# The last products of a two-branch FFT kernel, cut into eight tiles of the array (one core)

## The chip, the cores and the metric

The kernel runs on one core of a Trainium2 chip. The metric is the device time of one execution in microseconds (us), the median over runs. Everything is float32; inputs start in DRAM and the output ends there.

## The reference

`x` has 2048 time steps and 640 channels. Two branches are mixed by a gate with one value for each time step:

```python
def _A_ref(u, log_A_real, A_imag, C_real, C_imag, log_dt, D_skip):
    ...
    K = 2.0 * jnp.einsum("dn,dnl->dl", C, P).real
    L2 = 2 * L
    u_t = u.transpose(0, 2, 1)
    Kf = jnp.fft.rfft(K, L2)
    Uf = jnp.fft.rfft(u_t, L2)
    y = jnp.fft.irfft(Uf * Kf[None, :, :], L2)[:, :, :L]
    ...
    return y + u * D_skip[None, None, :]

def _B_ref(x, w_r, w_i):
    X = jnp.fft.rfft2(x, axes=(-2, -1)) * (w_r + 1j * w_i)
    return jnp.fft.irfft2(X, s=(S, D), axes=(-2, -1))

x = A_u
g = _sigmoid((x * gate_w).sum(-1, keepdims=True))
a = _A_ref(x, ...)
b = _B_ref(x, B_w_r, B_w_i)
return g * a + (1 - g) * b
```

Branch A is a causal convolution over time with a filter of 2048 taps for each channel (`P` holds exponentials of 128 modes), done by FFTs of length 4096. Branch B is a two-dimensional FFT filter over time and channels.

## The kernel before, in words

All FFTs are products with tables on TensorE, in two stages. The channels are taken in four quarters of 160, called `c`. Time is 32 blocks of 64 steps, so that an inverse transform ends with a small product: for each of the 64 steps of a block, the 32 blocks come from 64 rows (real and imaginary parts of the odd frequencies of a 64-point transform) or from 32 rows (the even ones).

**Ahead of the change** stand the phases up to about 440 us. `phase_a` transforms `x` over time and leaves its spectrum in DRAM (`u_d`), forms the gate (`T.gate`: partition, kind, 16 values), and filters branch B, which it leaves one product short in DRAM as `s3e_d[c]`, 32 rows of 64 steps by 160 channels. `phase_p` and `phase_b` compute the filter `K` beside it (products `p_k`, L690, whose tiles are 128 rows by 32 columns), and leave it in `k_d`.

**`phase_d`** is where the change lies. It loops over the quarters `c` = 0 to 3 and in each over five groups `g` of the 33 frequency pairs (four, four, four, four and one; in the last quarter the single one comes fourth). The program hands several streams of instructions to `merge`, which deals them out by their estimated costs, so that the order on each engine is fixed when the program is built. The streams of one step are:

- `mains` (4.8): load a group of the spectrum (`us`, on ScalarE's queue); `fronts`: stage 2 of the filter's transform (`p_s`, L345), then VectorE multiplies out of PSUM (`ma` L792, `mb` L793) and VectorE and GpSimd add the halves into `t2` (L797, L798); `backs`, two groups behind (one behind in the last five): the first inverse stage (`p_i`, L811), ScalarE's copy to `s3` (L813, L815), and the stores to DRAM `s3_d[c]` (L817 for the one row `s3_d[c, 33]`, L820 for the others, on ScalarE's queue).
- `some(fst, ...)` (2.1): stage 1 of the next quarter's filter (`p_s`, L332), copied by ScalarE (L333), with its loads (`load_k`).
- what stands beside (2.4 for each): `last_e(c, a)` and `last_c(c - 1, a)`, for `a` = 0 and 8, in the groups that the loop names. `last_e` finishes branch B for eight of the 16 steps that lie beside each other in a row: the product `p_e` of `t3e` with the table `T.e3e` (the helper `halved`, L157), then VectorE multiplies by 1 - g into `oe` (L872). `last_c` finishes branch A: the product `p_c` of `t3` with `T.e3` (L889), then VectorE multiplies by g into `ot` (L894) and GpSimd adds `oe` (L895). In the last quarter VectorE does both in one (L892).

The data of these products come back from DRAM. `load_e` (L851, SyncE's queue) brings `s3e_d[c]` as 128 rows: 32 rows times four groups `r` of 16 steps. `load_c` (L862, SyncE's queue but for one) brings rows `p` to `p + n` of `s3_d[c]` as 2n rows: each row times two halves `j` of 32 steps. In the first three quarters it is called with n = 32, in the last with n = 16, and the final one in two parts.

The tables `e3` (128 by 64) and `e3e` (128 by 128) are block diagonal: 128 rows meet 64 columns, and each column has values for 64 or 32 of the rows and zeros for the others. A step of eight is worked in pieces of three, three and two (480, 480 and 320 columns of data); a piece is two matmuls, one to each half of PSUM's partitions, into a slot of `pd` (two slots of one bank). `ps` (three slots of two banks) serves all the other products of `phase_d`.

`behind(T.mm)` places a product after the latest `p_i` matmul in the order. After the loop come the remaining `backs`, the last loads of `t3`, `last_c` of quarters 2 and 3, and the stores of the output (`out`, L897 on GpSimd's queue, L900 and L950 on SyncE's). On the host `_lay_back` brings the output into its order.

## Time and profile before

| what | value |
|---|---|
| time, three runs | 620.0, 618.89, 628.3 us; median 620.0 |
| the profiled execution's own time | 619.24 us |
| its span, first to last instruction | 617.4 us |
| mean granted TensorE clock | 0.955 |
| busy PE (matmul), PEld (weight load) | 537.5 us (87%), 407.1 us (66%) |
| busy DVE, ACT, POOL | 506.9 us (82%), 391.3 us (63%), 268.5 us (43%) |
| DMA | 101.98 MB in 47987 packets, mean 165 GB/s |

The shares are those of the whole span; `phase_d` fills its last 180 us or so. The page's slices and the rows of a stretch show the limits of that stage, which are others than those of the phases ahead. In the rows quoted below, PE is TensorE's matmul, PEld its weight load, DVE VectorE, ACT ScalarE, POOL GpSimd, SP SyncE; an ending q names an engine's queue. A float32 matmul leaves two records, one for each of its passes, so that a `x4` of PE in the chain or the timeline is two matmuls. "128*64" is the tile of the array that a matmul uses, rows by columns; "128x480" is data, partitions by elements. A group's line shows count, busy time and mean ns of one, then the idle time before its instructions and what ended it. Buffer numbers are left out of names there.

### The profile page before, as it was taken

What the parts mean: (1) busy time and instruction counts of PE and PEld (TensorE: products, weight loads), DVE (VectorE), ACT (ScalarE), POOL (GpSimd) and SP (SyncE); (2) the same over time, 40 slices, a digit from 0 to 9 for tenths busy, and PEclk for the clock granted to TensorE, in tenths of its full rate; (3) what the DMA queues carried; (4) which work ended last, traced back from release to release, by engine and by line L of the source; (5) the groups of instructions that cost most, each with busy time, mean ns of one, the idle gap of its engine ahead of it and who ended that gap; (6) DMA issues with size and microseconds to landing.
All of it is one profiled execution on the core that took longest, in us unless ns stands there. A gap on an engine that the chain in (4) does not pass through costs nothing. (4 is left out here: it accounts for less than half of the span.)

```text
span 617.4 us, 16697 instructions
## 1 busy us (share of the span) xinstructions
PE 537.5 (87%) x7084; PEld 407.1 (66%) x7084; DVE 506.9 (82%) x788; ACT 391.3 (63%) x659; POOL 268.5 (43%) x246
## 2 busy tenths in 40 slices
PE   8688979978978979989899989998789989998874
PEld 6577657756665757676667766666667768787641
DVE  5961798799799978998999998778297886986954
ACT  6667675566866777798699897799735324333110
POOL 4921262053346255365336335235253437456441
PEclk9889989979989998998999989899999999999978
DMA  8776203235612321333233032105966989899996
GB/s 339 301 289 230 88 7 137 76 109 200 242 56 66 96 85 25 94 120 124 76 108 95 2 125 79 48 26 158 333 242 225 302 218 370 243 282 289 251 240 212
DMA packets 47987, 101.98 MB, mean 165 GB/s; under 512 B 3220, under 2 KB 32680, under 8 KB 46152
## 3 DMA queue, kind: packets, MB, share of 16 engines
q1 hardware_dynamic: 24792, 67.74, 33.7%
q10 hardware_dynamic: 20080, 22.52, 11.7%
q0 software_dynamic: 3040, 10.65, 5.2%
q8 instruction: 56, 0.92, 0.6%
q14 instruction: 19, 0.16, 0.1%
HBM read 60.91 MB, written 39.98 MB: 163 GB/s over the span
## 5 line engine op out<-in xcount | busy, mean ns | idle before, releaser
L676 POOL TENSOR_TENSOR y<-e,sc 128x512 f32<-128x512 f32 x40 | 57.9, 1447 | 123.0 <-issue 61.7
L345 PE MATMUL p_s<-t,w 128*64 128x160 f32 x1056 | 88.5, 308 | 11.8 <-ACT t L333 4.2
L345 PEld LDWEIGHTS p_s<-t,w 128*64 128x64 f32 x1056 | 74.6, 140 | 21.1 <-ACT t L333 5.7
L637 ACT ACTIVATE e<-p_e 128x512 f32<-128x512 f32 x120 | 68.5, 601 | 24.1 <-PE p_e L635 21.8
L333 ACT COPY t<-p_s 128x512 f32<-128x512 f32 x40 | 44.7, 1141 | 61.5 <-PE p_s L332 43.3
L548 PE MATMUL p_eo<-td,pmt 107*128 107x321 f32 x204 | 68.9, 462 | 3.7 <-ACT pmt L502 3.7
L690 PE MATMUL p_k<-x,y 128*32 128x64 f32 x2560 | 61.9, 228 | 10.0 <-DVE x L675 5.4
L690 PEld LDWEIGHTS p_k<-x,y 128*32 128x32 f32 x2560 | 45.3, 113 | 37.5 <-issue 30.7
L649 DVE SCALAR_TENSOR_TENSOR q<-q,p_p 128x512 f32<-128x512 f32 x80 | 52.9, 680 | 12.4 <-ACT q L648 10.9
L635 PE MATMUL p_e<-rm,par 128*128 128x512 f32 x120 | 57.4, 510 | 4.1 <-ACT e L637 2.2
L677 POOL TENSOR_TENSOR y<-e,sc 128x512 f32<-128x512 f32 x40 | 55.2, 1380 | 4.4 <-ACT sc L663 4.4
L797 POOL TENSOR_TENSOR t<-ma 64x320 f32<-64x320 f32 x32 | 28.3, 883 | 64.0 <-DVE ma L792 52.7
L646 PE MATMUL p_p<-rp,par 128*128 128x512 f32 x80 | 44.5, 566 | 9.6 <-DVE q L649 9.4
L548 PEld LDWEIGHTS p_eo<-td,pmt 107*128 107x128 f32 x204 | 38.7, 199 | 19.8 <-ACT pmt L502 6.8
L811 PE MATMUL p_i<-t,w 128*64 128x160 f32 x528 | 45.0, 305 | 4.7 <-POOL t L798 3.2
L648 ACT ACTIVATE q<-p_p 128x512 f32<-128x512 f32 x80 | 46.4, 595 | 2.7 <-PE p_p L646 2.5
L332 PE MATMUL p_s<-c,u 128*64 128x128 f32 x640 | 44.2, 284 | 3.5 <-ACT ut L379 2.8
L332 PE MATMUL p_s<-c,kt 128*64 128x128 f32 x640 | 43.4, 275 | 3.9 <-DVE mb L793 1.6
L332 PEld LDWEIGHTS p_s<-c,kt 128*64 128x64 f32 x640 | 38.3, 137 | 13.0 <-issue 5.9
L792 DVE TENSOR_TENSOR ma<-p_s,us 128x640 f32<-128x640 f32 (+1 forms) x36 | 28.2, 783 | 21.9 <-PE p_s L345 14.1
L811 PEld LDWEIGHTS p_i<-t,w 128*64 128x64 f32 x528 | 38.2, 139 | 9.6 <-POOL t L798 4.1
L332 PEld LDWEIGHTS p_s<-c,u 128*64 128x64 f32 x640 | 36.8, 140 | 11.3 <-issue 5.1
(154 smaller groups left out, 1206.2 us busy)
## 6 DMA issues: line engine op xcount, KB each, us to landing
u_d<-ut SPq DMA_DIRECT2D x32, 320.0 KB, 2.7
us<-u_d ACTq DMA_DIRECT2D x16, 640.0 KB, 7.1
s_d<-s ACTq DMA_DIRECT2D x15, 640.0 KB, 8.6
t<-s_d SPq DMA_DIRECT2D x6, 1280.0 KB, 9.6
ww<-in_w_l SPq DMA_DIRECT2D x8, 642.0 KB, 3.9
ue<-u_d SPq DMA_DIRECT2D x8, 640.0 KB, 4.5
k_d<-kt SPq DMA_DIRECT2D x4, 1280.0 KB, 7.0
kt<-k_d SPq DMA_DIRECT2D x8, 640.0 KB, 6.4
```

Of the source, the lines that this page charges most:

```text
L332: nc.tensor.matmul(p[64 * ri:64 * ri + 64, j, :], src(i + j), e1[ri], start=True, stop=True)
L333: copy(dst[:, :, :, i:i + n], p[:, 0:n, :].rearrange("p q (j k) -> p j k q", j=4))
L345: ins = nc.tensor.matmul(p[64 * j:64 * j + 64, i, 160 * ri:160 * ri + 160], w2[:, x, 64 * ri:64 * ri + 64], t1[:, x if x < 32 else K0, :], ...
L548: P.matmul(p[:, :E], st.pmt[:DC, c, w, j, :], tv[:DC, w, c, :], start=c == 0, stop=c == 2)
L635: P.matmul(p[:, :], pars[t], rm[:, c:c + 512], start=True, stop=True)
L637: st.exp = S.activation(ef[:, c:c + 512], p[:, :], AF.Exp)
L648: S.activation(qf[:, c:c + 512], p[:, :], AF.Copy, bias=MAGIC)
L649: V.scalar_tensor_tensor(out=qf[:, c:c + 512], in0=qf[:, c:c + 512], scalar=MAGIC, in1=p[:, :], op0=ALU.subtract, op1=ALU.subtract)
L676: G.tensor_tensor(out=y[:, 1], in0=e[:, :, 64:96], in1=sc[:, 0], op=ALU.mult)
L677: G.tensor_tensor(out=y[:, 0], in0=e[:, :, 64:96], in1=sc[:, 1], op=ALU.mult)
L690: P.matmul(st.pb[32 * r:32 * r + 32, o, :], y[:, ri, 4 * qq + JR[r], :], x[:, ri, 4 * qq + JR[r], :], start=t % 2 + qq + 1 - ri == 0, stop ...
L811: T.mm = P.matmul(p[x:x + 64, i // 2, 160 * (i % 2):160 * (i % 2) + 160], T.w3[:, k0 + h + i, x:x + 64], t2[:, h + i, :], start=True, stop ...
```

## The change

The last two products use the array in eight tiles at once. A tile is 64 rows (branch A) or 32 rows (branch B) by 32 columns.

- The tables lose their zeros: `e3` and `e3e` are now 32 columns wide, and hold the same 64 rows twice and the same 32 rows four times.
- A new function `product` issues eight matmuls of 320 columns for a piece: for each of four column slots `s` (32 of PSUM's partitions) and two halves `j` (a bank each) the rows of half `j`, steps 4s + v and 4s + v + 1. A piece `v` = 0 or 2 gives 640 elements in each partition; a step of eight is two pieces, not three.
- `p_l`, the product's PSUM slot, comes from `ps`, which has four slots of two banks now. `pd` is gone.
- VectorE multiplies a whole piece (128 by 640) at once; in the last quarter it still works by 160.
- The halves `j` lie on partitions 0 to 63 and 64 to 127 of `t3` now (before: two neighbouring partitions for each row). So each load of `load_c` becomes two DMAs, one for each `j`, of n rows; `load_e` becomes four DMAs of 32 rows.
- The output's partitions are now (s, block) instead of (x, j, block), so `_lay_back`, the gate's copy and the views `four` and `gate` follow. The stores of the last quarter are one whole and two pieces of 320 KB, where they were one whole, one of six steps and one of two before.
- `yield 0.8` becomes `yield 1.2` in both streams, which shifts how `merge` deals them out.

```diff
-    e3 = np.zeros((64, 2, 2, 32))
-    for j in range(2):
-        e3[:, j, j, :] = kr
-    e3e = np.zeros((32, 4, 4, 32))
-    for r in range(4):
-        e3e[:, r, JR[r], :] = kr[32:64]
+    e3, e3e = np.tile(kr, (2, 1)), np.tile(kr[32:64], (4, 1))
...
-    y = y.reshape(4, 2, 2, 32, 16, 160)
-    return np.ascontiguousarray(y.transpose(3, 2, 1, 4, 0, 5).reshape(1, L, D))
+    y = y.reshape(4, 4, 32, 2, 2, 4, 160)
+    return np.ascontiguousarray(y.transpose(2, 4, 3, 1, 5, 0, 6).reshape(1, L, D))
...
-def halved(nc, out, w, x):
-    for i in (0, 64):
-        nc.tensor.matmul(out[i:i + 64], w[:, i:i + 64], x, start=True, stop=True)
...
-        T.e3, T.e3e, T.id, T.one = take(64), take(128), take(128), take(32)
+        T.e3, T.e3e, T.id, T.one = take(32), take(32), take(128), take(32)
...
-            V.tensor_copy(T.gate[32 * r:32 * r + 32, 0, :], p[32 * r:32 * r + 32, 16 * JR[r]:16 * JR[r] + 16])
+            o = slice(32 * r, 32 * r + 32)
+            V.tensor_copy(T.gate[o, 0, :].rearrange("p (x j v) -> p x j v", x=2, j=2), p[o].rearrange("p (j x s v) -> p x j s v", j=2, x=2, s=4)[:, :, :, r])
...
-    ps = ctx.enter_context(tc.tile_pool(name="c_ps", reuse_waits="tile", bufs=3, space=PSUM))
-    pd = ctx.enter_context(tc.tile_pool(name="d_ps", reuse_waits="tile", bufs=2, space=PSUM))
+    ps = ctx.enter_context(tc.tile_pool(name="c_ps", reuse_waits="tile", bufs=4, space=PSUM))
...
-        nc.sync.dma_start(t3es[c][:, :, :], T.s3e_d[c].rearrange("k (r a) d -> (k r) a d", r=4))
+        for r in range(4):
+            nc.sync.dma_start(t3es[c][32 * r:32 * r + 32], T.s3e_d[c, :, 16 * r:16 * r + 16])
...
-        src = T.s3_d[c, p:p + n].rearrange("k (j x a) d -> (k j) x a d", x=2, j=2)
-        w = 16 // parts
-        for a in range(0, 16, w):
-            T.ld = eng.dma_start(t3s[c][2 * p:2 * p + 2 * n, :, a:a + w], src[:, :, a:a + w])
+        src = T.s3_d[c, p:p + n].rearrange("k (j x a) d -> j k x a d", x=2, j=2)
+        for x in range(parts):
+            w = slice(x, x + 1) if parts > 1 else slice(0, 2)
+            for j in range(2):
+                T.ld = eng.dma_start(t3s[c][64 * j + p:64 * j + p + n, w], src[j, :, w])
+    def product(w, t, x, v, rows):
+        p = ps.tile([128, 2, 512], F32, tag="ps", name="p_l")
+        with behind(T.mm):
+            for s in range(4):
+                for j in range(2):
+                    r = slice(64 * j + rows[0], 64 * j + rows[1])
+                    P.matmul(p[32 * s:32 * s + 32, j, 0:320], w[r, :], t[r, 4 * s + v:4 * s + v + 2, :], start=True, stop=True)
+        return p[:, :, 0:320].rearrange("p j (v d) -> p j v d", v=2)
...
-        for i in range(0, AG, 3):
-            n = min(3, AG - i)
-            p = pd.tile([128, 3, 160], F32, tag="pd", name="p_e")
-            with behind(T.mm):
-                halved(nc, p[:, 0:n], T.e3e, t3es[c][:, a + i:a + i + n])
-            V.tensor_tensor(out=oe[:, i:i + n], in0=p[:, 0:n], in1=gate(1, a + i, n), op=ALU.mult)
-            yield 0.8
+        x = a // AG
+        for v in (0, 2):
+            p = product(T.e3e, t3es[c], x, v, (32 * x, 32 * x + 32))
+            V.tensor_tensor(out=four(oe, v), in0=p, in1=gate(1, a, v), op=ALU.mult)
+            yield 1.2
...
-        for i in range(0, AG, 3):
-            n = min(3, AG - i)
-            p = pd.tile([128, 3, 160], F32, tag="pd", name="p_c")
-            with behind(T.mm):
-                for x in range(2):
-                    P.matmul(p[64 * x:64 * x + 64, 0:n], T.e3, t3[:, x, a + i:a + i + n], start=True, stop=True)
+        x = a // AG
+        for v in (0, 2):
+            p = product(T.e3, t3[:, x], x, v, (0, 64))
...
-                V.tensor_tensor(out=ot[:, i:i + n], in0=p[:, 0:n], in1=gate(0, a + i, n), op=ALU.mult)
-                (V if c == 2 and a and n < 3 else G).tensor_tensor(out=ot[:, i:i + n], in0=ot[:, i:i + n], in1=oe[:, i:i + n], op=ALU.add)
-            if c < 2 and i + n == AG:
+                V.tensor_tensor(out=four(ot, v), in0=p, in1=gate(0, a, v), op=ALU.mult)
+                (V if c == 2 and a and v else G).tensor_tensor(out=four(ot, v), in0=four(ot, v), in1=four(oe, v), op=ALU.add)
+            if c < 2 and v:
                 G.dma_start(out[c, :, a:a + AG], ot[:, :, :])
-            elif c == 3 and i + n > (5 if a else 6):
-                x = i if a and i > 3 else 0
-                nc.sync.dma_start(out[c, :, a + x:a + i + n], ot[:, x:i + n])
-            yield 0.8
+            elif c == 3 and (v or a):
+                o = out[c, :, a:a + AG]
+                if a:
+                    nc.sync.dma_start(four(o, v), four(ot, v))
+                else:
+                    nc.sync.dma_start(o, ot[:, :, :])
+            yield 1.2
```

In the changed file `stage1` is L320, stage 2 L333, `p_i` L799, the products of `product` L866, `load_e` L845, `load_c` L857, the stores of `s3` L805 and L808, ScalarE's copies of it L801 and L803.

TensorE's order, a stretch in the middle of `phase_d` in which quarter 0's results are finished beside quarter 1's groups. The rows name the tiles `p_s` (both stages of the filter's transform), `p_i` (inverse stage) and `p_c` (branch A's product); a count is in matmuls here. Before:

```order
L345 MATMUL p_s_6280<-t_5652,w_68 64x160 x7
L889 MATMUL p_c<-t_6071,c_65 64x480 x2
L345 MATMUL p_s_6280<-t_5652,w_68 64x160
L889 MATMUL p_c<-t_6071,c_65 64x480 x2
L332 MATMUL p_s_6302<-c_65,kt 64x128 x8
L811 MATMUL p_i_6313<-t_6075,w_5306 64x160 x8
L889 MATMUL p_c<-t_6071,c_65 64x320 x2
L811 MATMUL p_i_6329<-t_6075,w_5306 64x160 x8
```

The three pieces of a step are single pairs of matmuls, each in one place. The same stretch now, with `p_l` for the product's tile:

```order
L333 MATMUL p_s_6284<-t_5652,w_68 64x160 x8
L866 MATMUL p_l<-t_6090,c_65 32x320
L320 MATMUL p_s_6313<-c_65,kt 64x128 x8
L333 MATMUL p_s_6323<-t_5652,w_68 64x160 x8
L320 MATMUL p_s_6340<-c_65,kt 64x128 x8
L799 MATMUL p_i_6351<-t_6095,w_5306 64x160 x8
L866 MATMUL p_l<-t_6090,c_65 32x320
L799 MATMUL p_i_6373<-t_6095,w_5306 64x160 x5
L866 MATMUL p_l<-t_6090,c_65 32x320 x14
L799 MATMUL p_i_6373<-t_6095,w_5306 64x160 x3
L333 MATMUL p_s_6392<-t_5652,w_68 64x160 x2
L866 MATMUL p_l<-t_6090,c_65 32x320 x8
```

The two products of a step have one matmul early and the other seven together, in the middle of another block of `p_i`. Counted over the loop, the rows of `p_l` form 28 groups. After the loop the remaining ones stand together.

SyncE's queue of DMAs from quarter 1's loads of `t3` to the end. Before:

```order
L862 DMA t_6495<-s_d 64x5120 x2
L851 DMA t3e<-s3e_d 128x2560
L862 DMA t_6894<-s_d 64x5120 x2
L862 DMA t_6975<-s_d 32x5120 x2
L862 DMA t_6975<-s_d 32x2x1280 x2
L950 DMA out<-ot 128x1280 x2
L900 DMA out<-ot 128x1280
L900 DMA out<-ot 128x960
L900 DMA out<-ot 128x320
```

The loads of `t3` go to 64 rows, those of the last quarter to 32, `t3e` to all 128. Now:

```order
L857 DMA t_6549<-s_d 32x5120 x4
L845 DMA t3e<-s3e_d 32x2560 x4
L857 DMA t_6983<-s_d 32x5120 x4
L857 DMA t_7074<-s_d 16x5120 x4
L857 DMA t_7074<-s_d 16x2560 x4
L955 DMA out<-ot 128x1280 x2
L905 DMA out<-ot 128x1280
L903 DMA out<-ot 128x2x320 x2
```

The order of the transfers stays; a load of 64 rows has become two of 32, one of 32 two of 16, one of 128 four of 32. On ScalarE's queue the rows stay as they were; its last DMA, 32 rows of `t3`, has become two of 16.

15 lines of the change are left out of this document (10 added, 5 removed).

## Prediction

> **What bounds** the kernel now. I read the stretches first: busy time of PE, DVE and the rest, TensorE clock, DMA share and GB/s.
>
> ```profile
> 480.00:500.00 20.00, 18.33 (x244) 14.98 (x242) 19.27 (x26) 7.11 (x8) 9.88 (x11) 1.00 0.87 247
> 520.00:540.00 20.00, 18.16 (x236) 14.82 (x238) 17.63 (x24) 7.28 (x9) 10.68 (x12) 1.00 0.91 286
> 560.00:580.00 20.00, 16.36 (x195) 12.98 (x196) 17.76 (x24) 4.00 (x6) 10.73 (x12) 1.00 1.00 295
> 580.00:600.00 20.00, 15.90 (x148) 10.86 (x146) 13.80 (x22) 4.35 (x7) 7.53 (x9) 0.83 0.95 235
> 600.00:617.40 17.40, 8.80 (x36) 2.52 (x32) 7.42 (x21) 0.00 (x0) 4.38 (x4) 0.86 0.67 208
> ```
>
> The columns after the length are PE, PEld, DVE, ACT and POOL. Until 580 us three resources are almost full together: PE has 16.4 to 18.3 of 20 us, DVE 17.6 to 19.3, the DMA engines 0.87 to 1.00. None can give back much alone. From 580 on PE and DVE thin out and the DMA engines stay at 0.95. The chain that ended last says who decides there:
>
> ```profile
> 575.53 10.79 DMA s_d<-s
> ...
> 587.72 6.40 DMA s_d<-s
> ...
> 597.11 2.77 DMA s_d<-s
> ...
> 599.94 5.88 DMA t<-s_d
> ...
> 605.95 3.96 PE p_c L889 x12
> ```
>
> From 575.5 to 605.8 the path is mostly transfers: stores of `s3` to DRAM (`s_d`), then the load of the last quarter of `t3`. A store takes 2.77 us for half a tile alone, but 10.79 and 6.40 us for whole ones while `t3` loads run. So two prices matter: the products on PE and DVE before 594 us, and the loads after 575 us.
>
> **The products on PE.** Today's costs, from the chain inside the loop and from the groups by line:
>
> ```profile
> 537.27 0.87 PE p_s L332 x16
> ...
> 539.23 0.81 PE p_e L157 x4
> ...
> 541.99 0.54 PE p_e L157 x4
> ```
>
> ```profile
> L889 PE MATMUL p_c<-t,c 128*64 128x480 f32 (+1 forms) x96 | 25.7, 602 | 8.5 <-DVE t L798 3.8 <-DMA t<-s_d 3.7 <-PE p_c L889 0.6
> L157 PE MATMUL p_e<-t3e,c 128*64 128x480 f32 (+1 forms) x96 | 21.9, 529 | 4.6 <-DVE oe L872 4.6
> L690 PE MATMUL p_k<-x,y 128*32 128x64 f32 x2560 | 61.9, 228 | 10.0 <-DVE x L675 5.4 <-issue 2.1 <-ACT kt L698 1.8
> ```
>
> Four records (two matmuls, two passes each) of 480 columns hold PE 0.81 us, of 320 columns 0.54 us. One step of eight channels costs 0.81 + 0.81 + 0.54 = 2.16 us. Each line has 96 records, so eight such steps. Twelve of the sixteen stand inside the loop: 25.9 us.
>
> After, a run of up to eight matmuls of 320 columns should cost 0.54 us if all eight overlap, 1.08 us for a step. But the order splits them. Counting the rows of `L866` inside the loop gives 31 runs (fourteen in a row count as two) in 28 groups with `128*64` matmuls around them. The runs cost 31 x 0.54 = 16.7 us. Each group changes the array's tiles twice. A change of that kind stands in the trace where `p_k` (32 columns wide) stands between `p_s` (64):
>
> ```profile
> 432.88 1.09 PE L332 MATMUL p_s<-c,kt 128*64 128x128 f32 x16 [0.34 <-ACT t L333]
> 433.90 1.10 PE L690 MATMUL p_k<-x,y 128*32 128x64 f32 x64
> 435.06 2.06 PE L332 MATMUL p_s<-c,kt 128*64 128x128 f32 x32
> ```
>
> Sixteen `p_s` records need 0.87 us from start to next start; here 433.90 - 432.88 = 1.02, so 0.15 us is lost on the way in. The `p_k` row is 1.10 us long with its last record's 0.22 (mean 228 ns), so `p_s` could follow after 0.88; it follows after 1.16: 0.28 us. I take 0.4 us of these 0.43 for a round trip, since the second may hold a short wait. 28 x 0.4 = 11.2 us. PE inside the loop: 16.7 + 11.2 - 25.9 = +2.0 us. If changing tiles were free it would be -9.2; if the row tiles did not overlap, 16.7 more than my value. No row shows row tiles overlapping; four column tiles do, since 64 `p_k` records go by in 0.88 us, 14 ns each. I take the overlap.
>
> **The products on DVE.**
>
> ```profile
> L792 DVE TENSOR_TENSOR ma<-p_s,us 128x640 f32<-128x640 f32 x32 | 26.3, 821 | 21.4 <-PE p_s L345 14.1 <-issue 5.7 <-POOL t L798 1.3
> L872 DVE TENSOR_TENSOR oe<-p_e,gate 128x480 f32<-128x480 f32 x16 | 10.5, 657 | 0.5
> L894 DVE TENSOR_TENSOR ot<-p_c,gate 128x480 f32<-128x480 f32 x12 | 7.9, 655 | 11.4 <-PE p_c L889 9.0 <-issue 2.1
> L892 DVE SCALAR_TENSOR_TENSOR ot<-p_c,gate,oe 128x160 f32<-128x160 f32 x16 | 5.0, 377 | 5.8 <-PE p_c L889 5.7
> L872 DVE TENSOR_TENSOR oe<-p_e,gate 128x320 f32<-128x320 f32 x8 | 3.8, 481 | 0.0
> L894 DVE TENSOR_TENSOR ot<-p_c,gate 128x320 f32<-128x320 f32 x6 | 2.9, 488 | 3.7 <-PE p_c L889 3.7
> ```
>
> The gate multiplications fall from 42 to 28, each of 640 elements. `ma`, also 640 out of PSUM, takes 0.821: 28 x 0.821 = 23.0 us for 10.5 + 7.9 + 3.8 + 2.9 = 25.1, so -2.1 us. With both engines full I let both count: +2.0 - 2.1 = 0 for the loop. POOL's additions become fewer and longer under 11 us of 20 busy: nothing; on a critical add it would be well under 1 us.
>
> **The PSUM ring.** Five slots (three of two banks, two of one) become four of two banks shared by all. PE's wait for `oe`, 4.6 us, may vanish. Against that, where the first matmul of two products is issued early (three places), they hold two of four slots for some five blocks of about 1 us, and PE may wait for one evacuation, about 1 us, once or twice: up to +4. I take 0.
>
> **The loads.** Bytes stay, the rows of each transfer change, and the rate depends on them (last column, GB/s):
>
> ```profile
> 452.00:454.00 2.00, 0.94 (x18) 0.97 (x20) 1.97 (x4) 0.00 (x0) 1.66 (x2) 1.00 1.01 425
> 541.50:544.50 3.00, 3.00 (x44) 2.63 (x42) 2.94 (x5) 2.26 (x3) 1.55 (x2) 1.00 1.08 218
> 602.50:603.50 1.00, 0.00 (x0) 0.00 (x0) 0.79 (x2) 0.00 (x0) 1.00 (x2) 1.00 0.98 195
> 606.50:608.50 2.00, 2.00 (x8) 0.54 (x4) 0.65 (x3) 0.00 (x0) 0.00 (x0) 0.50 1.00 417
> ```
>
> In 452:454 `t3e` and `us` load to 128 rows, in 606.5:608.5 128 rows are stored: 417 to 425. In 541.5:544.5 a `t3` load goes to 64 rows, in 602.5:603.5 the last ones to 32: 218 and 195, with the engines just as busy. So half the array's rows halve the rate, and a quarter costs no more.
>
> `t3e` now comes as four loads of 32 rows: 1280 KB need 6.2 us at 213 GB/s, not 3.1, four times.
>
> ```profile
> 519.64 19.25 SPq L862 DMA_DIRECT2D t<-s_d  x2
> ...
> 542.57 0.33 SPq L851 DMA_DIRECT2D t3e<-s3e_d  x1
> ```
>
> ```profile
> 566.53 0.97 PE L157 MATMUL p_e<-t3e,c 128*64 128x480 f32 x4
> ```
>
> ```profile
> ACT s L813 <- DMA s_d<-s: 8.2, 2, 5.2
> ```
>
> The load issued at 542.57 is first read at 566.53, 24 us later, which hides 3.1 us. What it could reach are the stores beside it, and ACT waited for stores only twice, both after 575 us: 0, at most +3 if that cover goes. The two halves of a 64-row `t3` load become a low and a high pair of 32 rows, one behind the other: same rate if the engines keep step, better if they drift; 0, at best -2.
>
> The last channel's `t3` loads fall from 32 rows to 16 + 16. No row shows 16. Between the rates of 32 rows (195 to 213, no loss) and half of them (107, if the next halving costs what the first did) a 640 KB load takes 3.1 to 6.2 us. By the nearest row alone it is 3.1; I take the middle, 4.7, because one of two known halvings did cost. Two of these loads run while the store of 587.72 waits, and that store lies on the path: ACT's next store writes a DRAM row of the same range, so ACT stands until it lands, and behind it queue the last three stores, two evacuations and a load. 2 x 1.6 = +3.1 us, between 0 and +9 (the second rival). The final loads, 5.88 us on the chain: +1, between 0 and +2.
>
> The Trainium skill, page SBUF — State Buffer, section Door 1: The DMA port swizzle, says that rows 0 to 31 and 0 to 63 both reach 8 of 16 ports, as the trace has it, and rows 0 to 15 only 4, with 104 GB/s measured; no run here shows 16 rows. By it alone the sum would be the second rival's.
>
> **The finish.** DVE sets it:
>
> ```profile
> 607.85 0.97 DVE L892 SCALAR_TENSOR_TENSOR ot<-p_c,gate,oe 128x160 f32<-128x160 f32 x3 [4.53 <-PE p_c L889]
> 609.40 1.55 DVE L892 SCALAR_TENSOR_TENSOR ot<-p_c,gate,oe 128x160 f32<-128x160 f32 x5 [0.57 <-PE p_c L889]
> 611.53 2.59 DVE L892 SCALAR_TENSOR_TENSOR ot<-p_c,gate,oe 128x160 f32<-128x160 f32 x8 [0.58 <-PE p_c L889]
> ```
>
> ```profile
> out<-ot SPq DMA_DIRECT2D x1, 480.0 KB, 2.6
> out<-ot SPq DMA_DIRECT2D x1, 160.0 KB, 2.3
> ```
>
> PE starts at 605.95 and DVE at 607.85. At the slow clock of that moment a product takes about 1.1 us, so DVE starts near 607.25, and then has 0.97 + 1.55 + 2.59 = 5.1 us without a gap: 612.4 instead of 614.1, -1.7. The last store grows from 160 to 320 KB: +0.3 at most.
>
> **Sum.** The profiled execution took 619.24 us (span 617.4). 0 (loop) + 3.1 + 1 (loads) - 1.7 + 0.3 = +2.7: 622 us. The execution lies 0.8 us under the runs' median of 620.0, so as a ratio this is 1.00. Two per cent, 12.4 us, is about what a measurement of this kernel tells from no change (its runs spread from 618.9 to 628.3).
>
> **Rivals.** First, gain: changing tiles costs far less than 0.4 us. PE gives back up to 9.2 us in the loop, DVE 2.1; DVE's 17.6 to 19.3 of 20 leave room for about half, 5 to 6, and with -1.4 at the end and no loss in the loads it is 612. For it: the chain holds `p_e` and `p_c` again and again. Against: the two rows above, and the split products.
>
> Second, the starved store, slower: 16-row loads at 107 GB/s take 6.2 us. The place is the store of 587.72. The first load runs from about 588, the second stands right behind it in the same queue before the store is through, and the store gets its turn only after both: 588 + 12.4 + 2 = 602.5 instead of 594.1, +8.4; final loads +2, finish -1.4: 628. It decides from the point where the second load is queued before the first ends. For it: 10.79 us for the first store, behind `t3`. The skill's page above, by its 104 GB/s, gives this rival.
>
> Third, row tiles do not overlap: +16.7 in the loop, 639. The Trainium skill, page TensorE: Matmul & The Clock Gate, Part 3, reports row and column tiles running at once; no run here shows it, and by it this rival falls.
>
> **Chances.** 622 (616 to 627) 0.52; starved store 0.27; gain 0.15; no overlap 0.06. Range 611 to 631: it cuts off half of the gain, the end of the starved store and the third rival. Slower by over 2% (above 631.6): 0.12; faster (below 606.8): 0.04; within: 0.84.
>
> **What would show it.** PE records of `p_l` a few ns apart in eights, about 0.54 us from group to group: overlap right. About 0.15 us lost before and 0.28 us after each group: switching right. GB/s near 210 while `t3e` loads, and 105 to 160 under the 16-row loads. The second-last whole store taking 9 to 10 us instead of 6.40. The last DVE instruction about 6.5 us after the first `p_l` of the last eight. I am wrong if the loop (first `p_e` to the end of the last `p_i`) shortens by over 5 us, or if the stores after 575 us are no slower than now.

## The result, and the profile after

The changed kernel takes 643.58 us (median of 6 runs, 636.12 to 651.88); the kernel before took 624.57 us in the runs beside it. The ratio is 1.030, with a 95% interval from 1.020 to 1.040. The forecast was 622 us, no change, with a range that ended at 631. The change makes the kernel slower by 3%.

The profiled execution takes 636.12 us with a span of 634.3 us. The phases ahead of the change took as long as before: the first `ma` starts at 445.3 us, before at 444.9. All of the difference, 189.0 - 172.5 = 16.5 us, lies in `phase_d`. First its stretches, as in the prediction (length, then PE, PEld, DVE, ACT, POOL, TensorE clock, DMA share, GB/s):

```profile
480.00:500.00 20.00, 17.93 (x286) 15.13 (x288) 17.35 (x22) 8.39 (x10) 9.32 (x10) 1.00 1.01 289
520.00:540.00 20.00, 19.03 (x314) 15.97 (x312) 15.31 (x23) 10.15 (x12) 14.33 (x14) 1.00 1.03 330
560.00:580.00 20.00, 17.40 (x276) 14.18 (x260) 15.21 (x22) 5.39 (x8) 14.52 (x15) 1.00 1.02 298
580.00:600.00 20.00, 14.24 (x186) 11.92 (x184) 16.39 (x23) 4.94 (x8) 8.05 (x10) 0.91 0.88 230
600.00:620.00 20.00, 5.86 (x70) 2.44 (x66) 4.20 (x5) 0.69 (x1) 5.10 (x3) 0.74 0.91 146
620.00:634.30 14.30, 4.36 (x64) 2.31 (x64) 4.76 (x16) 0.00 (x0) 0.00 (x0) 0.62 0.69 215
```

Up to 580 us PE and DVE are about as full as before, and the DMA engines a little fuller (1.01 to 1.03 for 0.87 to 1.00). Then stands a stretch that before did not have: from 600 to 620 us no compute engine is busy for more than 5.9 of the 20 us, the DMA engines are 0.91 busy, and they move 146 GB/s. The chain that ended last names it:

```profile
564.54 16.98 DMA s_d<-s
...
588.58 6.57 DMA s_d<-s
...
596.65 6.50 DMA s_d<-s
...
603.22 4.94 DMA s_d<-s
...
608.26 9.48 DMA t<-s_d
...
617.76 5.79 DMA t<-s_d
623.55 2.43 PE p_l L866 x17
...
626.00 2.13 DVE ot L894 x7
...
628.42 2.33 DVE ot L894 x8
```

Where before had one `t3` load of 5.88 us on the chain, there are now 9.48 + 5.79 = 15.3 us. The whole stores of 588.58 and 596.65 hold the rows of those that before issued at 583.42 and 587.72; they take 6.57 and 6.50 us, and that of 587.72 took 6.40. But they come later: from the last `ma` to the issue of the load on the chain are 608.26 - 595.1 = 13.2 us, before 599.94 - 590.5 = 9.4. The store of 564.54, which heads the fence, took 16.98 us; the same rows took 14.1 us before (issued at 559.5).

For what follows, `phase_d` is cut at the first `ma` of each quarter; the tail runs from the start of the last `ma` to the end of the span. These pieces stand for one profiled execution each, because the phases ahead of `phase_d`, which are the same in all kernels, differ by up to 15 us between executions (their first `ma` starts between 442.8 and 458.0 us); they are differences of times shown to 0.1 us. The totals are compared by the ratio to the kernel before on the same chip. Some executions of every kernel are longer, at a lower granted clock: the ratios leave them out, and the eight profiles that are such executions (loads_alone, count_alone, t3e_narrow, products_late, t3e_home, two_queues, own_ring, before_spread) start their first `ma` at 452.2 us or later, the others at 449.3 or earlier.

| kernel | quarter 0 | 1 | 2 | 3 | tail | sum, us | ratio to before (95%) |
|---|---|---|---|---|---|---|---|
| before | 35.0 | 41.8 | 40.8 | 28.0 | 26.9 | 172.5 | 1 |
| after | 37.0 | 45.8 | 38.9 | 28.0 | 39.2 | 189.0 | 1.030 (1.020 to 1.040) |
| loads_alone | 37.3 | 43.6 | 45.5 | 32.9 | 42.0 | 201.3 | 1.049 (1.033 to 1.064) |
| count_alone | 35.2 | 44.4 | 40.3 | 28.0 | 26.0 | 173.9 | 1.009 (1.003 to 1.015) |
| t3e_narrow | 37.3 | 45.6 | 39.9 | 28.0 | 30.7 | 181.5 | 1.011 (1.004 to 1.018) |
| products_alone | 37.9 | 43.5 | 43.0 | 28.0 | 27.0 | 179.3 | 1.009 (1.004 to 1.013) |
| products_late | 35.6 | 42.3 | 44.1 | 28.0 | 26.9 | 177.0 | 1.009 (1.003 to 1.014) |
| t3e_home | 36.7 | 44.6 | 39.4 | 28.5 | 32.5 | 181.7 | 1.013 (1.009 to 1.018) |
| spread_split | 38.2 | 47.2 | 39.0 | 28.0 | 28.2 | 180.6 | 1.014 (1.001 to 1.027) |
| two_queues | 38.3 | 47.4 | 39.3 | 28.0 | 31.3 | 184.3 | 1.011 (1.006 to 1.017) |
| own_ring | 36.1 | 41.6 | 46.4 | 34.1 | 33.2 | 191.4 | 1.024 (1.016 to 1.032) |
| e_wide | 35.6 | 42.8 | 39.4 | 28.6 | 26.3 | 172.8 | 0.991 (0.986 to 0.996) |
| before_spread | 35.0 | 39.5 | 39.4 | 28.0 | 24.9 | 166.7 | 0.983 (0.978 to 0.989) |
| spread_pieces | 38.5 | 38.4 | 38.1 | 28.1 | 22.2 | 165.3 | 0.984 (0.977 to 0.990) |
| pieces_late | 35.6 | 38.3 | 38.1 | 28.1 | 24.2 | 164.3 | 0.984 (0.978 to 0.990) |
| products_spread | 35.6 | 37.9 | 37.7 | 28.0 | 22.9 | 162.1 | 0.980 (0.974 to 0.985) |

So +2.0 and +4.0 us in quarters 0 and 1, -1.9 in quarter 2, and +12.3 in the tail: 3.7 up to the issue of the load on the chain, 9.4 in the loads, -0.8 behind them.

The products themselves behave as hoped. Rows of PE in quarter 1 and the groups of the changed kernel:

```profile
500.90 0.77 PE L866 MATMUL p_l<-t3e,c 32*32 32x320 f32 x16 [0.26 <-DVE oe L875]
501.60 1.31 PE L799 MATMUL p_i<-t,w 128*64 128x160 f32 x16
502.74 1.26 PE L333 MATMUL p_s<-t,w 128*64 128x160 f32 x16
510.06 1.24 PE L866 MATMUL p_l<-t,c 64*32 64x320 f32 x2 [6.06 <-issue]
```

```profile
L866 PE MATMUL p_l<-t,c 64*32 64x320 f32 x256 | 18.9, 517 | 25.3 <-DMA t<-s_d 16.0 <-issue 6.1 <-ACT s L801 3.0
L866 PE MATMUL p_l<-t3e,c 32*32 32x320 f32 x256 | 14.2, 439 | 4.3 <-DVE oe L875 2.6 <-DVE mb L781 1.5
L875 DVE TENSOR_TENSOR oe<-p_l,gate 128x640 f32<-128x640 f32 x16 | 13.1, 824 | 1.8 <-PE p_l L866 1.4
L896 DVE TENSOR_TENSOR ot<-p_l,gate 128x640 f32<-128x640 f32 x12 | 9.6, 819 | 17.9 <-PE p_l L866 16.6 <-issue 1.3
```

Sixteen records, a whole piece of eight matmuls, hold PE from 500.90 to 501.60: 0.70 us, where the two row tiles one after the other would take 1.08. Row tiles do overlap. But the last row of the first fence shows a single matmul of a product at 510.06 before which PE stood 6.06 us. Before, the first product of branch A in that quarter had this:

```profile
507.30 1.39 PE L889 MATMUL p_c<-t,c 128*64 128x480 f32 x5 [2.33 <-DVE t L798]
```

The views name no load as releaser here; in the built program both wait for `t3`. Its last loads of quarter 0 were issued at 502.63 and 502.97 us, when a one-row store had landed after 7.5 us; before, the load was issued at 497.63, behind a store of 3.7 us, and landed at 507.21. The 3.7 us more of waiting are about what quarter 1 lost.

### The profile page after: what moved, and what is told of

The parts are those of the page before. It is cut to its first block, busy times and chain, and to the rows that moved or that the text cites. A ratio compares the mean times of both kernels' runs of the same rounds, so it can differ in the third digit from the quotient of the medians.

```text
span 634.3 us, 17351 instructions
## 1 busy us (share of the span) xinstructions
PE 536.0 (85%) x7404; PEld 403.4 (64%) x7404; DVE 504.2 (79%) x774; ACT 391.8 (62%) x659; POOL 266.9 (42%) x240
## 4 chain that ended last, share of the span: by engine, by line
PE 40%; DVE 23%; DMA 11%; ACT 11%; issue 3%; ACTq 0%; DVEq 0%
PE p_eo L537 7%; DMA s_d<-s 6%; PE p_s L333 5%; PE p_k L679 4%; PE p_s L320 4%; PE p_e L624 3%; DMA t<-s_d 3%; PE p_i L799 3%; PE p_d L504 3%; PE p_l L866 3%; PE p_d L505 2%; ACT t L321 2%; DVE q L638 2%; ACT q L637 2%; DVE t L786 2%
## 5 line engine op out<-in xcount | busy, mean ns | idle before, releaser
L333 PE MATMUL p_s<-t,w 128*64 128x160 f32 x1056 | 89.9, 312 | 14.4 <-ACT ut L367 4.7
L333 PEld LDWEIGHTS p_s<-t,w 128*64 128x64 f32 x1056 | 75.5, 142 | 25.4 <-ACT ut L367 5.6
L638 DVE SCALAR_TENSOR_TENSOR q<-q,p_p 128x512 f32<-128x512 f32 x80 | 53.2, 682 | 12.4 <-ACT q L637 10.8
L537 PEld LDWEIGHTS p_eo<-td,pmt 107*128 107x128 f32 x204 | 39.3, 203 | 20.2 <-ACT pmt L491 6.8
L801 ACT COPY s<-p_i 128x640 f32<-128x640 f32 x32 | 21.6, 694 | 45.7 <-PE p_i L799 18.1
L637 ACT ACTIVATE q<-p_p 128x512 f32<-128x512 f32 x80 | 46.4, 595 | 4.8 <-PE p_p L635 4.5
L780 DVE TENSOR_TENSOR ma<-p_s,us 128x640 f32<-128x640 f32 (+1 forms) x36 | 28.2, 783 | 25.6 <-PE p_s L333 17.9
L320 PE MATMUL p_s<-c,u 128*64 128x128 f32 x640 | 44.4, 285 | 3.9 <-ACT ut L367 2.9
L799 PE MATMUL p_i<-t,w 128*64 128x160 f32 x528 | 44.3, 310 | 3.9 <-issue 3.3
L320 PE MATMUL p_s<-c,kt 128*64 128x128 f32 x640 | 43.1, 279 | 4.9 <-issue 2.0
L320 PEld LDWEIGHTS p_s<-c,kt 128*64 128x64 f32 x640 | 36.6, 139 | 12.6 <-issue 5.3
L320 PEld LDWEIGHTS p_s<-c,u 128*64 128x64 f32 x640 | 37.1, 141 | 11.7 <-issue 5.2
```

Source lines behind the costliest of these rows:

```text
L320: nc.tensor.matmul(p[64 * ri:64 * ri + 64, j, :], src(i + j), e1[ri], start=True, stop=True)
L333: ins = nc.tensor.matmul(p[64 * j:64 * j + 64, i, 160 * ri:160 * ri + 160], w2[:, x, 64 * ri:64 * ri + 64], t1[:, x if x < 32 else K0, :], ...
L537: P.matmul(p[:, :E], st.pmt[:DC, c, w, j, :], tv[:DC, w, c, :], start=c == 0, stop=c == 2)
L637: S.activation(qf[:, c:c + 512], p[:, :], AF.Copy, bias=MAGIC)
L638: V.scalar_tensor_tensor(out=qf[:, c:c + 512], in0=qf[:, c:c + 512], scalar=MAGIC, in1=p[:, :], op0=ALU.subtract, op1=ALU.subtract)
L799: T.mm = P.matmul(p[x:x + 64, i // 2, 160 * (i % 2):160 * (i % 2) + 160], T.w3[:, k0 + h + i, x:x + 64], t2[:, h + i, :], start=True, stop ...
```

## The experiments

Three theories were held against each other: **rows** (narrow transfers move fewer bytes a second), **count** (23 more transfers wait for each other; the expectations say 20), **products** (changes of the array's tiles, the shared slots, the new order).

**loads_alone**: the loads of the change in the kernel before.

```diff
-        e3[:, j, j, :] = kr
+        e3[j, :, j, :] = kr
...
-        e3e[:, r, JR[r], :] = kr[32:64]
+        e3e[r, :, JR[r], :] = kr[32:64]
...
-        nc.sync.dma_start(t3es[c][:, :, :], T.s3e_d[c].rearrange("k (r a) d -> (k r) a d", r=4))
+        for r in range(4):
+            nc.sync.dma_start(t3es[c][32 * r:32 * r + 32], T.s3e_d[c, :, 16 * r:16 * r + 16])
-            T.ld = eng.dma_start(t3s[c][2 * p:2 * p + 2 * n, :, a:a + w], src[:, :, a:a + w])
+            for j in range(2):
+                T.ld = eng.dma_start(t3s[c][64 * j + p:64 * j + p + n, :, a:a + w], src[j, :, :, a:a + w])
```

> The kernel before, with only the loads of the change: t3e in four transfers of 32 rows, each t3 load in two of 32 (16 in the last quarter) rows, with the rows of the zero-padded tables put in the matching order. Products, PSUM pools and order stay. Change against before is 636.1 - 619.2 = +17 us between the profiled executions. Rows theory (narrow transfers move fewer bytes a second) and count theory (20 more transfers, each of which stands in its queue until an unrelated earlier one has landed): +12 to +18 us, about 634, with the last load of t3 landing 12 us or more after the last store of s3 was issued. Products theory (tile changes, the shared PSUM slots and the new order cost the time): within 4 us of before.

Measured: 1.049 of before, some 30 us, with a tail of 42.0 us. The products are not needed for the loss; rows or count make it. It is more than the whole change loses. The program's order on PE differs here (the builder placed branch B's products a group later), so this is no pure sum of the parts. In its tail all four 640 KB loads of the last quarter are issued from 625.97 us on, beside or behind the last store (626.50); in the change there are three. The rest of the excess was not settled.

**count_alone**: as many transfers, none narrower.

```diff
+        for a in range(0, 16, 4):
+            nc.sync.dma_start(t3es[c][:, a:a + 4], src[:, a:a + 4])
...
+            for x in range(2):
+                T.ld = eng.dma_start(t3s[c][2 * p:2 * p + 2 * n, x, a:a + w], src[:, x, a:a + w])
```

> The kernel before, with as many transfers as the change has but none on fewer rows: t3e in four transfers of 128 rows by 4 steps, each t3 load in two of the same 64 (32) rows by half the steps. Count theory: most of the loss, +8 to +17 us, with a t3e transfer that is issued only when an earlier transfer of another queue has landed, as in the change at 515.27. Rows theory: at most +3 us, since every transfer covers the rows that it covered before. Products theory: no change.

Measured: 1.009, and 173.9 us in `phase_d`. As many transfers cost little here. But the builder, which turns the kernel into each engine's list of instructions, gives all transfers of SyncE's and ScalarE's queues eight semaphores in turn (counters that a landed transfer raises). So one waits for the transfer that had its semaphore before, and which one that is depends on the exact number and order of transfers. In the change it is one that matters. The second of the 16-row loads carries a wait for one such semaphore and for nothing else in the built program:

```
138 L857 DMA t3_7074<-s3_d_59 16x5120 [waits DMAHW1_49]
```

Its own rows had been stored at 584.06. In the trace (the timeline of that line alone) it is issued at 603.2, as the store of 596.65 lands (+ 6.50 = 603.15):

```profile
L857 SPq DMA_DIRECT2D t<-s_d x1: 302/302/302, 603.2 to 603.2; - x1
```

The next two 16-row loads in that queue wait in the same way for the stores of 603.22 and 603.80. They are issued at 608.18 and 609.00, though the rows that they read had landed with the store of 588.58, at 595.15. count_alone, in which the semaphores come round otherwise, could not show this.

**spread_split**: the same transfers with their rows spread.

```diff
-                T.ld = eng.dma_start(t3s[c][64 * j + p:64 * j + p + n, w], src[j, :, w])
+                T.ld = eng.dma_start(t3s[c][64 * j + p // n:64 * j + 64:64 // n, w], src[j, :, w])
```

> The changed kernel with the same transfers in the same number, but the rows of t3 spread: a transfer of 32 rows takes every second row of a half of 64, one of 16 rows every fourth (the table's rows are put in that order). Rows theory, by the extent of the rows: the last loads of t3 run at about 200 GB/s and no longer at 130 to 150, -8 to -12 us against the change, about 633 on the scale where the change has 643. If it is the number of rows and not their extent, or count or products theory: within 3 us of the change.

Measured: 1.014 for the change's 1.030; the tail falls from 39.2 to 28.2 us. Number of transfers, bytes, rows in each, order on every engine and waits are those of the change: only the place of the rows differs. (The intervals of the two ratios overlap a little; the tail and the rates carry the reading.) The stretches of the last loads, in the changed kernel and here:

```profile
612.00:617.00 5.00, 0.00 (x0) 0.00 (x0) 0.00 (x0) 0.00 (x0) 0.14 (x1) 0.60 1.02 131
```

```profile
607.00:609.50 2.50, 0.31 (x7) 0.00 (x0) 2.43 (x3) 0.00 (x0) 2.50 (x3) 0.92 1.05 229
```

Only 16-row loads are in flight in both. The DMA engines are busy all the time, and move 131 and 229 GB/s. So 16 neighbouring rows are slow by their extent, not by their number, and "busy" does not say how much is moved.

**one_load**: products of the change, one transfer for each load.

```diff
+        nc.sync.dma_start(t3es[c][:, :, :], T.s3e_d[c].rearrange("k (r a) d -> r k (a d)", r=4))
...
+            T.ld = eng.dma_start(t3s[c][p // n:128:64 // n, w], src[:, :, w])
```

> The changed kernel's products, but one transfer for each load: t3e to all 128 rows at once, t3 to 64 rows two apart or 32 rows four apart over all 128 (the table's rows in that order). The number of transfers is that of before. Rows theory and count theory: all of the loss goes, 620 or less; if the extent of the rows sets the rate, a load of 64 rows takes 3 to 4 us and not 6, and the tail after the last store of s3 shortens by some 4 us below before's 20: 610 to 616. Products theory: 636 or more.

Measured: 1.320. Every theory was wrong about it.

```profile
784.00:789.00 5.00, 0.00 (x0) 0.00 (x0) 0.00 (x0) 0.00 (x0) 0.00 (x0) 0.50 0.13 51
```

The source's outermost dimension is now the half `j`, of size 2, and the DMA share is 0.13 = 2/16: two of the sixteen DMA engines carry the load, at 51 GB/s. The Trainium skill, page DMA: Bandwidth & Descriptors, section Why a DMA increments its semaphore by 16 and not by 1, states the rule: the number of engines is the largest up to 16 that divides the slowest dimensions of both sides. The trace agrees.

**before_spread**: the kernel before, with spread rows and the outermost dimension unchanged.

```diff
+    e3 = np.concatenate([e3.reshape(m, 64 // m, 2, 64).transpose(1, 2, 0, 3).reshape(128, 64) for m in (2, 4)], 1)
...
-            T.ld = eng.dma_start(t3s[c][2 * p:2 * p + 2 * n, :, a:a + w], src[:, :, a:a + w])
+            T.ld = eng.dma_start(t3s[c][p // n:128:64 // n, :, a:a + w], src[:, :, a:a + w])
```

> The kernel before, with one thing changed: a load of t3 of 64 rows takes every second of all 128 rows, one of 32 rows every fourth (the zero-padded table's rows in that order). Number of transfers, products and order on every engine are those of before. The theory that the extent of the rows sets the rate (a load over 64 neighbouring rows 218 GB/s, over 16 129 GB/s, over 128 417 GB/s in the profiles) says: a whole t3 load takes 3 to 4 us and not 6 once it runs, the stage from the first ma to the end falls from 172.5 to 164 to 169 us, and the time to 611 to 617 where before has 620. If only very narrow loads are slow, or if the stores are what fills the transfer engines: within 3 us of before.

Measured: 0.983, `phase_d` 166.7 us. The stretch of a load of 64 rows two apart:

```profile
585.00:588.00 3.00, 3.00 (x32) 2.00 (x30) 2.97 (x5) 0.00 (x0) 1.86 (x2) 1.00 0.91 324
```

In before, the stretch of a load of 64 neighbouring rows moved 218 GB/s (541.5 to 544.5, in the prediction); transfers of 128 rows run beside the load in both. The second load of quarter 2 took 10.7 us from issue to landing in before, and 6.4 us here. The order on every engine is that of before. The rows' extent had cost the kernel before, too.

**two_queues**: the last 16-row loads of one half on ScalarE's queue.

```diff
+                T.ld = (nc.scalar if eng is nc.scalar and j else nc.sync).dma_start(
...
-    load_c(3, 48, 16, 2)
+    load_c(3, 48, 16, 2, eng=nc.scalar)
```

> spread_split, with the last loads of t3 (the 16-row ones after the loop) of one half of the rows on SyncE's queue and of the other half on ScalarE's, so that both halves can move at once. Extent theory: the loads after the last store run at 300 GB/s or more, not 215 to 235, and the tail from the last ma to the end falls from 28.2 to about 25.5 us; the total by 2 to 3 us from spread_split. If the transfer engines are the limit and not the rows: no change.

Measured: 1.011, not to be told from spread_split's 1.014; the tail was 31.3 us. The gain that was expected did not come.

**e_wide**: spread_split, with branch B's product padded with zeros again and `t3e` on 128 rows.

```diff
+        for y in range(4):
+            nc.sync.dma_start(t3es[c][:, 4 * y:4 * y + 4], src[y])
...
+                for i in (0, 64):
+                    for j in range(2):
+                        o = 8 * j + 4 * x + v
+                        P.matmul(p[i:i + 64, j, 0:320], T.e3e[:, i:i + 64], t3es[c][:, o:o + 2], start=True, stop=True)
```

> spread_split, with branch B's product as it was: a table with zeros, 128 rows by 64 columns, four matmuls of 320 columns for a piece, and t3e in four transfers of all 128 rows each (not 32). PE pays 8 pieces of 1.08 us and not 0.80 in each pair of quarters, about +4.5 us of its time in all. What is left of the loss in spread_split stands in the first two quarters (first ma of one quarter to that of the next: 38.2 and 47.1 us, before 34.9 and 41.9). If the narrow t3e loads make it, by delaying the stores and t3 loads beside them: the first two quarters fall to 36 and 43 and the time by 4 to 7 us from spread_split. If the products or the shared slots make it: no change or slower.

Measured: 0.991, and 35.6 and 42.8 us in quarters 0 and 1 (38.2 and 47.2 in spread_split). It has as many transfers, pays more of PE's time and is 2.3 points faster. That is what the narrow `t3e` loads were expected to cost. But the order on PE differs too, and with it the waits: the late pair of 16-row loads waits for its own rows here.

**own_ring**: spread_split, with one slot of its own for `p_l`.

```diff
-    ps = ctx.enter_context(tc.tile_pool(name="c_ps", reuse_waits="tile", bufs=4, space=PSUM))
+    ps = ctx.enter_context(tc.tile_pool(name="c_ps", reuse_waits="tile", bufs=3, space=PSUM))
+    pl = ctx.enter_context(tc.tile_pool(name="d_ps", reuse_waits="tile", bufs=1, space=PSUM))
```

> spread_split, with a slot of its own (one, of two banks) for the product p_l and three for the other products, where four were shared. If products that are issued one matmul early hold slots that the filter's stages lack, the first two quarters fall from 38.2 and 47.1 us towards 34.9 and 41.9: 4 to 7 us less. If the loads make the loss: within 2 us of spread_split, or slower, since a single slot lets no piece begin before the one ahead is read.

Measured: 1.024. Quarters 0 and 1 do fall, to 36.1 and 41.6 us, but quarters 2 and 3 rise by 7.4 and 6.1. It does not separate the slots from the order that comes with them; as a remedy it fails.

**products_alone**: the change with the loads of before (the products then meet rows of other steps).

```diff
-        for r in range(4):
-            nc.sync.dma_start(t3es[c][32 * r:32 * r + 32], T.s3e_d[c, :, 16 * r:16 * r + 16])
+        nc.sync.dma_start(t3es[c][:, :, :], T.s3e_d[c].rearrange("k (r a) d -> (k r) a d", r=4))
...
-            for j in range(2):
-                T.ld = eng.dma_start(t3s[c][64 * j + p:64 * j + p + n, w], src[j, :, w])
+            T.ld = eng.dma_start(t3s[c][2 * p:2 * p + 2 * n, w], src[:, w])
```

> The changed kernel with the loads as they were before: t3e in one transfer to 128 rows, t3 in transfers of 64 (32) rows, at their old places. The products then meet rows that belong to other steps, so what it computes is not the output wanted; instructions, sizes and transfers are those of the question. It tells what the products, the shared slots and the new order are worth without the loads. If the loads make the whole loss, the stage from the first ma to the end is 172.5 us (before) or less: with PE's measured 0.80 us for a piece of eight matmuls and 14 fewer instructions on DVE 169 to 172, and the time 0.98 to 1.00 of before. Products theory: 176 or more.

Measured: 1.009, 179.3 us. So the loads of before, with the slightly other order that the builder makes for them, take back 9.7 of the 16.5 us, and 6.8 stay: the expectation of 172 us or less was wrong, and the mark of the products theory, 176 or more, is met. Among the waits of quarter 0 (us in all, times, longest) one names a reason:

```profile
PE p_l L864 <- DMA t3e<-s3e_d: 3.0, 1, 3.0
```

The first piece stands two blocks earlier in PE's order than before, and PE stands 3.0 us for `t3e` there.

**t3e_home**: the change with `t3e` alone loaded as before (the edit is the first half of the one above).

> The changed kernel with t3e alone loaded as before, one transfer to 128 rows (branch B's product then meets rows of other steps, and its part of the output is not the one wanted). t3's loads are those of the change, 32 and 16 rows. If the narrow t3e loads cost about 8 us in the first two quarters, as e_wide against spread_split says, the stage from the first ma to the end falls from 189.0 to about 181 us with a tail that stays near 39. If e_wide gained by something else (its product with zeros keeps the tile of the array): within 2 us of the change.

Measured: 1.013 for 1.030, `phase_d` 181.7 us, 7.3 less. The size was as expected, the place was not: 6.7 us are in the tail, which was to stay, so the size was met by luck. The second pair of 16-row loads shows where, first in the changed kernel, then here, each followed by the last two stores on ScalarE's queue:

```profile
L857 SPq DMA_DIRECT2D t<-s_d x2: 302/504/705, 608.2 to 609.0; - x2
```

```profile
L808 ACTq DMA_DIRECT2D s_d<-s x2: 544/1466/2389, 603.8 to 605.1; - x2
```

```profile
L856 SPq DMA_DIRECT2D t<-s_d x2: 303/369/435, 611.3 to 611.7; - x2
```

```profile
L808 ACTq DMA_DIRECT2D s_d<-s x2: 366/456/545, 611.9 to 613.3; - x2
```

In the change the pair is issued 3 us after the last store, here ahead of it. So three of the four 640 KB loads of the last quarter are left behind the stores in the change, and two here, as before. In the built program the reason is not the rate of `t3e`'s loads: with twelve transfers fewer the semaphores come round otherwise, and this pair now waits for the store of its own rows (603.20, landed at 611.27). Quarters 0 and 1 gain 1.5 us alone; the first piece waits 2.8 us for `t3e` here, as in products_alone.

**t3e_narrow**: the kernel before with `t3e` alone in four loads of 32 rows (the edit is the `t3e` part of loads_alone).

> The kernel before with t3e alone loaded as in the change, four transfers of 32 rows (the table's rows in that order). If narrow t3e loads cost what they seem to, the stage from the first ma to the end rises from 172.5 to about 180 us, most of it in the first two quarters, and the time to about 1.013 of before. If they are hidden, as they lie 24 us ahead of their first use: within 2 us of before.

Measured: 1.011, 181.5 us, which is 9.0 us and 1.1 points more than before: 2.3 and 3.8 us in quarters 0 and 1, 3.7 in the tail. But the builder changed the order here as in loads_alone: branch B's first product stands 78 matmuls later on PE than before. So what the loads cost by their rows, without the order and the semaphores, no run isolates; t3e_home, t3e_narrow and e_wide give 7.3, 9.0 and 7.8 us with them. What the rows do to a transfer beside them does show. This is the stretch of the first `t3e` loads in the changed kernel, and the load of `us` beside it (the timeline of that one line, in the change and in the kernel before):

```profile
452.50:457.00 4.50, 3.37 (x40) 2.37 (x42) 4.44 (x7) 0.68 (x1) 2.83 (x4) 1.00 1.00 214
```

```profile
L767 ACTq DMA_DIRECT2D us<-u_d x1: 365/365/365, 450.2 to 450.2; - x1
...
DMA to landing us min/median/max: 11.4/11.4/11.4
```

```profile
L779 ACTq DMA_DIRECT2D us<-u_d x1: 327/327/327, 449.7 to 449.7; - x1
...
DMA to landing us min/median/max: 7.4/7.4/7.4
```

The same 640 KB take 4 us longer to land, beside DMA engines that are as full and move 214 GB/s where they moved 425 in the stretch of before that the prediction quotes.

**spread_pieces**: before_spread with the pieces of the change (four steps, shared slots of two banks), still padded with zeros.

```diff
-        for i in range(0, AG, 3):
+        for i in range(0, AG, 4):
+            p = ps.tile([128, 2, 512], F32, tag="ps", name="p_e")
+            with behind(T.mm):
+                for h in range(2):
+                    halved(nc, p[:, h, 0:320], T.e3e, t3es[c][:, a + i + 2 * h:a + i + 2 * h + 2])
```

> before_spread, with the change's pieces of four steps (640 elements for each VectorE instruction, 28 multiplications and not 42, slots of two banks shared by four) but with the zero-padded products, which need no narrow rows. PE pays the same 2.16 us for eight steps. If the fewer VectorE instructions are worth something once the loads are not in the way: 1 to 3 us below before_spread's 0.983 of before. If early products that hold shared slots cost it: no change or up to 3 us slower.

Measured: 0.984, the same as before_spread within the intervals; quarter 0 is 38.5 us, with the same wait for `t3e` as in products_alone, 3.1 us:

```profile
PE p_e L158 <- DMA t3e<-s3e_d: 3.1, 1, 3.1
```

These products use the 128*64 tile of before, so the early piece belongs to the pieces and slots, not to the smaller tiles. Its chain ends with one `t3` load of 3.54 us, where before had 5.88 and the change 15.3:

```profile
591.55 2.53 DMA s_d<-s
594.13 3.54 DMA t<-s_d
...
597.81 3.97 PE p_c L890 x16
601.81 2.43 DVE ot L893 x8
```

**pieces_late**, **products_late** and **products_spread** follow up what products_alone had left. One line delays the first piece:

```diff
+        if c + a == 0:
+            yield 1.2
```

> spread_pieces, with the first piece of branch B's first product two blocks later in PE's order (behind the first p_i block, where before had it about), by one more step of the stream ahead of it. If the wait of 3.1 us for t3e is what the first quarter lost, that quarter falls from 38.5 to about 35.5 us, and the time by 2 to 3 us from spread_pieces, to 0.979 of before. If the work simply moves: no change.

> products_alone with the same delay of the first piece (loads at their old places, so that rows of other steps are multiplied and the output is not the one wanted). If the early piece makes the loss that is left, the first quarter falls from 37.9 to about 35 us and the time from 1.009 to about 1.004 of before or less. If the changes of the array's tiles (28 groups, 0.26 us each beyond the bare 0.54) make it: 1.007 or more.

products_spread is products_late with the loads of before_spread:

```diff
-            T.ld = eng.dma_start(t3s[c][2 * p:2 * p + 2 * n, w], src[:, w])
+            T.ld = eng.dma_start(t3s[c][p // n:128:64 // n, w], src[:, w])
```

> products_late with t3's loads spread over all rows as in before_spread (output not the one wanted, as there). On equal loads and with pieces of the same size, the products without zeros should pay PE 0.80 us for a piece and not 1.08, 28 x 0.28 = 7.8 us in the loop. If PE were what the loop waits for: 4 to 8 us below pieces_late. If VectorE and the transfers set it: within 2 us of pieces_late.

Measured: the delay gives quarter 0 back in both (38.5 to 35.6, 37.9 to 35.6 us), but the totals do not move beyond their intervals (0.984 to 0.984, 1.009 to 1.009). What keeps products_late at 1.009 is `t3`: PE stands twice in front of a product, 2.9 and 4.5 us. The second, and the two stretches of that kernel in which VectorE is full:

```profile
558.44 1.32 PE L864 MATMUL p_l<-t,c 64*32 64x320 f32 x14 [4.50 <-DMA t<-s_d]
```

```profile
455.00:475.00 20.00, 16.00 (x254) 12.99 (x252) 19.66 (x26) 7.59 (x8) 10.37 (x13) 1.00 0.71 256
535.00:555.00 20.00, 16.95 (x260) 12.28 (x256) 19.66 (x26) 7.24 (x9) 10.21 (x11) 1.00 0.79 218
```

The expectation had put 1.007 or more down to the changes of the array's tiles. But products_spread has the same changes: with spread loads PE's waits for `t3` are gone and the same products come to 0.980 (0.974 to 0.985). That is 2.2 us less in `phase_d` than pieces_late, whose loads and pieces are the same and whose products are padded; the ratios do not separate the two. That a faster PE runs into VectorE fits the 19.66 of 20 us above, but in products_spread the same two stretches have 19.43 and 16.63; it was not tested.

## Why the prediction was wrong

**The loop's PE time** was right in its mechanism and its size was near. A piece of eight costs 0.70 us, some 0.10 us on the way in (a block of sixteen `p_s` records takes 1.19 us from 487.09 to the start of a piece, elsewhere 1.09) and 0.05 on the way out (0.92 for 0.87), 0.85 together, where the forecast had 0.54 + 0.40 = 0.94. Row tiles overlap, which the Trainium skill, page TensorE: Matmul & The Clock Gate, Part 3, had said; the third rival falls.

**VectorE's price** was right: 0.824 and 0.819 us for the forecast's 0.821.

**The step that failed is "The loads".** It failed in three ways.

- "The load issued at 542.57 is first read at 566.53, 24 us later, which hides 3.1 us." The distance hides latency. But the DMA engines were 0.87 to 1.00 busy, a row that the prediction itself had quoted, and the other transfers wait: by an estimate from the two rates, four loads at 214 GB/s for 425 take 4 x 3.1 = 12.4 us more of all sixteen engines, and a `us` load beside them landed 4 us later. The sum had 0 (at most +3). t3e_home, t3e_narrow and e_wide measure 7.3 to 9.0 us of `phase_d`, with a changed order and changed waits in each; 6.7 us of t3e_home's lie in the tail, where a pair of `t3` loads no longer waits for the last stores.
- The 16-row rate was right: 131 GB/s, 5.0 us for 640 KB, where the sum had 4.7. How many of these loads stand after the last store was wrong. The sum had two as before, with +1 us; three were left, 3 x 5.0 = 15 us, and the chain shows 15.3 for 5.88: +9.4. A pair that was to run beside the stores had slid behind them, because in the built program it waits for two stores whose rows it does not read (count_alone); with other waits it is issued ahead of them (t3e_home). The prediction had asked what the rows do to a transfer, not which transfers the 23 new ones would wait for. At 229 GB/s, behind the same waits, the tail is 11.0 us shorter (spread_split).
- The price was put on the store of 587.72 (+3.1). That store took 6.50 us for 6.40, and by the prediction's own last sign, stores no slower than now, it was wrong. The store that did get longer is that of 564.54, 16.98 us for 14.1, beside loads of 32 rows, and the stores behind it came 3.7 us later in the tail; whether it made them late was not tested. The second rival, 628 us, had the mechanism (16-row loads) and the side right, a rate near enough (107), and the place wrong: the final loads paid, not the store of 587.72. The Trainium skill, page SBUF — State Buffer, section Door 1: The DMA port swizzle, named there, gives 104 GB/s for rows 0 to 15; here 131 were measured, with loads to both halves of the rows in flight. By its rule that the rows' numbers decide how many ports a transfer reaches, 16 rows four apart reach twice as many as 16 neighbours; spread_split agrees (229 GB/s for 131).

**The PSUM ring**: +0 was taken with up to +4 as bound. In products_alone, early pieces cost about 2.3 us in quarter 0 (37.9 against 35.6 in products_late). So the early issue matters by what it waits for; what the held slots cost was not separated. PE's 6.06 us in quarter 1 of the changed kernel (before 2.33) are no such case: there the loads came later.

**The finish**: from the last products to VectorE's end was to take 6.5 us. VectorE's last row in the timeline:

```profile
626.00 4.76 DVE L894 SCALAR_TENSOR_TENSOR ot<-p_l,gate,oe 128x160 f32<-128x160 f32 x16 [15.24 <-PE p_l L866]
```

From 623.55 (the chain) to 626.00 + 4.76 = 630.76 are 7.2 us, without a gap between the sixteen instructions, as forecast. From the last load's landing to the end it is 0.8 us less than before, where the sum had 1.4.

Together: the loads make some two thirds of the loss. Without the new products they lose 1.049 (loads_alone), and with the loads of before the change stands at 1.009 instead of 1.030 (products_alone). Of the 16.5 us in `phase_d`, 9.7 go with the loads and 6.8 stay. Of those 6.8, 2.3 are the early piece, and in products_late PE waits twice for `t3`. Among the loads the rate of the 16-row ones is shown by spread_split (8.4 us of `phase_d` with nothing else changed). The shares of `t3e`'s rows, of the waits for unrelated stores and of the order are not shown and stay open, since no run changes one of them alone. e_wide comes to 172.8 us, but with spread `t3` loads, which are faster than those of before (5.8 us in before_spread).

## What to carry to other kernels

Where the DMA engines are full, cost a transfer by the engine time that it takes, however far ahead of its use it is issued; look at GB/s beside the DMA share, since a full share at 130 GB/s and one at 420 look alike. When a change adds transfers, read in the built program which earlier transfer each one waits for: here a pair of loads waited for two stores whose rows it did not read. When a product's layout is changed to save TensorE time, count what the new rows do to its loads first: here the products won 2.2 us of `phase_d` on equal loads, and the loads cost 9.7. The rows of a tile are free to choose if the table's rows follow; spreading them over all partitions, with a large dimension outermost, gave 1.7% by itself, and before_spread, spread_pieces and pieces_late all beat both kernels.
